# A fused sigmoid-attention and token-mixing kernel: eight load buffers instead of six, a re-planned instruction order, and the last output block in two PSUM banks

## The chip, the cores and the metric

The kernel runs on one core of a Trainium2 chip. The metric is device time in microseconds (us); lower is better. The core has five engines with queues of their own: PE (matrix multiplications; its weight loads are listed as PEld), DVE and ACT (element-wise work), POOL (element-wise work in SBUF) and SP (here it only issues DMAs). Work on one engine runs in program order; engines wait for one another through semaphores. PE writes PSUM, which has eight banks; DVE and ACT read PSUM and write SBUF.

## What is computed

```
scores = q @ k^T / sqrt(64) - log(448)      # 8 batches, 12 heads, 448 rows, 64 columns
attn   = sigmoid(scores)                    # no row sum: each element by itself
x      = attn @ v                           # -> 8 x 448 x 768, heads side by side
W      = (x @ w_q) @ (x @ w_k)^T / sqrt(64) # 448 x 448 for each batch
out    = relu(W @ x) @ w_out                # 8 x 448 x 768
```

The kernel computes W @ x as (x w_q) times ((x w_k)^T x), so that the 448 x 448 matrix is never formed. Inputs and output are float32 in HBM; the matrix work is done in bfloat16.

## The kernel before

**Tiling.** The 96 heads form 24 quads of four heads, three quads to a batch. A quad has q, k and v tiles of 128 x 896 float32 (448 KB each). Each is loaded by one SP DMA into a buffer of the pool `p_ld`, cast to bfloat16 (mostly on POOL, lines 178 and 188; a few on DVE), and q and k are brought into a transposed layout, by PE transposes with a copy out of PSUM (lines 202, 210, 272, 267) or by DVE transposes of SBUF tiles (lines 242, 249, 218).

**The stages, by the letter that stands for them.** `S` is one score step, 168 in all (seven for a quad): four PE matmuls into a pair of PSUM banks (line 284) and one ACT sigmoid over 128 x 896 elements (line 289). `P`/`p` is one step of attn @ v (line 302); after seven of them the sum leaves PSUM on DVE or, with the small letter, on ACT (line 311). `x`, `X`, `y` transpose the result (lines 325 and 342), `W`, `w`, `L`, `l` project it (six for a batch; `L` and `l` as four 64 x 64 matmuls whose halves are added afterwards, line 376; `W` and `w` as one 128 x 128 matmul, line 381), `N` and `U`/`T` form (x w_k)^T x, `M`/`m` multiplies by x w_q with the relu (line 438 on ACT, line 440 on DVE), and `O`, `o`, `I`, `i` are parts of the output product with w_out (lines 497, 534, 576), whose blocks are copied out of PSUM and stored to HBM. `F` is a filler matmul on zeros. Small letters mostly mean that the copy behind a step goes to ACT instead of DVE.

**Order.** All engines are ordered by hand: the string `PLAN` is read letter by letter, and each letter emits its instructions on all engines at once. No scheduler moves them afterwards. `PLAN` was made by a planner outside the kernel.

**Loads.** The string `ORDER` lists the loads. A load is issued as soon as the buffer that it reuses has been cast: `pump_loads` holds back load n until load n-6 has been cast, so six loads are under way or waiting at most. A dot ahead of a name gives its cast to DVE. Outputs are issued by SP too, in the same program order, so a load can stand behind an output that waits for its copy.

**PSUM.** Four pairs of banks are handed out from a free list. `bank1` gives one bank, `bank2` a pair. A block of `out_chunk` takes one bank: six matmuls of 128 x 384, then the copy. The last block of the kernel is copied by both engines: DVE takes 192 columns (line 597), ACT the other 192 (line 598), out of the same bank.

**Instruction streams.** PE's program is 7,464 weight loads and matmuls. DMA queue q8 brings it in pieces of 16 KB, 29 of them in this execution.

Of the kernel before, what the change touches and what calls it, by code (L numbers as in the profile page):

```python
# [17 lines left out]
def kernel(  # L18
# [12 lines left out]
    nc = tc.nc  # L31
# [6 lines left out]
    NU = B  # L38
    NJ = H // 4
    NC = D // P  # L40
    NB = D // 2
# [6 lines left out]
    def pool(name, bufs, **kw):  # L48
        return ctx.enter_context(tc.tile_pool(name=name, bufs=bufs, **kw))

    singles = pool("singles", 1)
    p_ld = pool("ld", 6)
    p_c16 = pool("c16", 2)
    p_v16 = pool("v16", 4)
    p_qk = pool("qk", 8)
# [16 lines left out]
    def bank2():  # L72
        n = free2.pop(0)
        return n, pairs[n], pairs16[n]

    def bank1():
        if halves:
            n, b = halves.pop(0)
        else:
            n, b = free2.pop(0), 0  # L80
            halves.append((n, 1))
        return (n, b), pairs[n][:, b], pairs16[n][:, b]

    def release(fb):
        if isinstance(fb, int):
            free2.append(fb)
        elif (fb[0], 1 - fb[1]) in halves:
            halves.remove((fb[0], 1 - fb[1]))
            free2.append(fb[0])
        else:  # L90
            halves.append(fb)
# [18 lines left out]
    def xt(u, j):  # L110
# [4 lines left out]


    PLAN = (
        "FFSSFKSSFqSFSkFSFFSFSPSappSPpSbSPPSSFqSSXSPSkSPppSprpSPPpSsP"
        "pPSXSPPSllSLzlLSPLpSpPSPPPSxSNSqkSUSpPSMpSppPSPSXSqkPSPppSWW"
        "SPPPSXSwMcSSwWWSppSPdxSpPPNSPSqkSMSSUpSpPSpMppSPSoSXSqkSOSMS"  # L120
        "ooMSSroopSsPPpSCPPPSooSzxOSOSLLcLSllLSpPpSpCpPdPSSOOSSoNxSOS"
        "xcSdUSPppSpPpSrPSoOSCPpSPsSPPpzSPOXoSMlLCSllLSLPpSpPPcpSPSdC"
        "OOSCSoXoSpMPScPppPSPSoOSxSdOXSppSppPpSPNooSMSUcdoSllxSLlLSLP"
        "pSPpPScPPodSoSMOSOSOrSOSMooPPsPSPxmpPPOSOSSOSzOOOSoNSOSUSPPx"
        "SpPMcpSppdllllScpPPpdLSlPOopSPooMeoSOSoSOOmoxSoNoSfTgPPSpppS"
        "POSPomOSOSooSoSOpSpPPSpocmepPoSooMlSLdLLSlLSOOSfgOSOSOoSxoSo"
        "PPxpSPpPSPoSoxSoSOSooSoNSOSTPpPSppSPPppMPppmpPylLlMLyllxiiiN"
        "iiUiimimImiiIoooOooOoOoooOooO"
    )
    PLAN = "".join(PLAN)  # L130
    KIND = ["a"] + [t for t in PLAN if t in "qacer"]
# [1 line left out]
    ld = {}  # L133
# [21 lines left out]
    def load1(n, nm, eng):  # L155
        u, j = quads[n]
        if KIND[n] in "cer" and nm != "v":
            t = p_ld.tile([P, 2 * NI * HD], F32, tag="ld", name=nm + "32")
            eng.dma_start(
                out=t, in_=SRC[nm][u, 4 * j : 4 * j + 4].rearrange("h (p r) d -> (h p) (r d)", r=2 * NI),  # L160
            )
            ld[nm, n] = t
            return
        t = p_ld.tile([P, 2, NI * HD], F32, tag="ld", name=nm + "32")
        eng.dma_start(
            out=t,
            in_=SRC[nm][u, 4 * j : 4 * j + 4].rearrange(
                "(g h) (p i) d -> (h p) g (i d)", g=2, i=NI
            ),
        )  # L170
        ld[nm, n] = t
# [304 lines left out]
    chunks = []  # L476
# [81 lines left out]
    def out_chunk(act, tail):  # L558

        if opened:  # L560
            w, m, nb, fb, ps = opened.pop()
            part = 1
        else:
            w, m, nb = chunks.pop(0)
            if nb < 0:
                nb = 0
                chunks.insert(0, (w, m, 1))
            fb, ps, _ = bank1()
            part = 0
        if nb == 0 and not part:  # L570
            ot[0] = p_o.tile([P, D], F32, tag="o", name="o")
        o = ot[0]

        def block(ps, w0, w1, c0, c1):
            for c in range(c0, c1):
                nc.tensor.matmul(  # L576
                    ps, mxs[w][:, 2 * S * c + m * P : 2 * S * c + (m + 1) * P],
                    wout16[:, c, w0:w1], start=(c == 0), stop=(c == NC - 1),
                )

        def store(cols):
            for y in range(2):
                b, i = divmod(2 * m + y, NI)
                eng = nc.scalar if tail and y else nc.sync
                eng.dma_start(
                    out=out[2 * w + b].rearrange("(p i) d -> p i d", i=NI)[:, i, cols],
                    in_=o[HALF[y], cols],
                )

        ps = ps[:, 0:NB] if not part else ps  # L590
        block(ps, nb * NB, (nb + 1) * NB, part * NC // 2, (part + 1) * NC // 2)
        if not part:
            opened.append((w, m, nb, fb, ps))
            return
        if w == NU // 2 - 1 and not chunks:
            h = NB // 2
            nc.vector.tensor_copy(out=o[:, NB : NB + h], in_=ps[:, 0:h])
            nc.scalar.copy(out=o[:, NB + h :], in_=ps[:, h:])
        else:
            COPY["s" if act else "v"](out=o[:, nb * NB : (nb + 1) * NB], in_=ps)  # L600
        release(fb)
        split = tail and w == NU // 2 - 1 and m == NI - 1
        if nb or split:
            store(slice(nb * NB, (nb + 1) * NB) if split else slice(0, D))
# [3 lines left out]
    def load_weights():  # L608
        w32["qk"] = p_ld.tile([P, 2 * NI * HD], F32, tag="ld", name="w32")[:, 0:D]
        for x, w in enumerate((moe_w_q, moe_w_k)):  # L610
            nc.sync.dma_start(
                out=w32["qk"].rearrange("p (c n) -> p c n", c=NC)[:, :, 64 * x : 64 * x + 64],
                in_=w.rearrange("(c p) n -> p c n", p=P)
            )

    def load_wout(c):
        w32[c] = p_ld.tile([P, 2 * NI * HD], F32, tag="ld", name="w32")[:, 0:D]
        nc.sync.dma_start(out=w32[c], in_=moe_w_out[c * P : (c + 1) * P, :])
# [9 lines left out]
    def cols(r):  # L628
        return slice(r.start * HD, r.stop * HD)
# [8 lines left out]
        out=ident, in_=ident, compare_op=ALU.not_equal, fill=1.0, base=0,  # L638
# [8 lines left out]
    for t in wqks:  # L647
# [1 line left out]


    ORDER = (
# [5 lines left out]
    )  # L657
    BY = {"s": [], "v": []}
    for x in ORDER.split():
# [9 lines left out]
    used, loaded, cast = set(), set(), set()  # L669

    ring = [("q", 0), ("k", 0)]

    def pump_loads():
        while len(loaded) < len(ORDER):
            nm, n = ORDER[len(loaded)]
            if len(ring) >= 6 and ring[-6] not in cast:
                break
            ring.append((nm, n))
            if nm == "w":
                load_wout(n - 1) if n else load_weights()  # L680
            else:
                load1(n, nm, nc.sync)
            loaded.add((nm, n))
            issued[nm, n] = done["S"]
# [55 lines left out]
    for t16, t32, r, e in ((q016, q0, IA, "v"), (q016, q0, IB, "s"), (k016, k0, KA, "g"), (k016, k0, KB, "g")):  # L740
        COPY[e](
            out=t16[:, r].rearrange("p i b d -> p b i d"),
            in_=t32[:, :, cols(r)].rearrange("p b (i d) -> p b i d", d=HD),
# [24 lines left out]
    for t in PLAN:  # L768
# [4 lines left out]
        c = done[kind]  # L773
# [29 lines left out]
        elif t == "K":  # L803
            tr_part("k", k016, KB, "v")
        elif kind == "x":
            tr_x(c, tail, t in "XY", "s" if t in "yY" else "v")
        elif kind == "W":
            mlp_wqk(*divmod(c, NC), tail, t in "wl", t in "Ll")
        elif kind == "C":
            for y in range(2):  # L810
                nc.sync.dma_start(out=wout16[HALF[y], NC + c, :], in_=wout16[HALF[1 - y], c, :])
        elif kind == "N":
            mlp_wkn(c)
        elif kind == "U":
            (mlp_tmp_tiled if t in "Tt" else mlp_tmp)(c, t in "ut")
        elif kind == "M":
            u, x = divmod(c, NC // 2)
            mlp_mix(u, x, t == "m", tail)
            if x == NC // 2 - 1:
                if u // 2 in TW:  # L820
                    chunks.extend((u // 2, ((u % 2, i), (u % 2, 6 - i))) for i in range(3))
                    if u % 2:
                        chunks.append((u // 2, ((0, 3), (1, 3))))
                else:
                    chunks.extend((u // 2, m, -1) for m in (range(3, NI) if u % 2 else range(3)))
        elif kind == "O":
            if (opened or chunks)[0][0] in TW:
                out_pair(t == "o")
            elif t in "Ii":
                out_halves(t == "i")  # L830
            else:
                out_chunk(t == "o", tail)
# [29 lines left out]
```

## Time and profile before

| what | value |
|---|---|
| median of 3 runs | 190.4 us (189.7 to 190.98) |
| profiled execution, its own time | 189.52 us |
| span of the profile in it | 187.7 us, so 1.82 us lie around it |
| PE busy | 175.9 us (94%) |
| ACT busy | 165.1 us (88%), of this 141.0 in 168 sigmoids |
| DVE / POOL busy | 137.8 us / 108.4 us |
| first sigmoid starts, last one ends | 6.62 us, 165.07 us |
| last matmul group (line 576) | 175.53 to 183.50 us |

Busy time says how long an engine had work under way; idle time is put down to what ended it (the releaser). "issue" as a releaser means that the engine waited for nothing that the profile shows. The chain of work that ended last is followed back from the end: at each step to what released it.

### The profile page before, as it was taken

What the parts mean: (1) busy time and instruction counts of PE and PEld (TensorE: products, weight loads), DVE (VectorE), ACT (ScalarE), POOL (GpSimd) and SP (SyncE); (2) the same over time, 40 slices, a digit from 0 to 9 for tenths busy, and PEclk for the clock granted to TensorE, in tenths of its full rate; (3) what the DMA queues carried; (4) which work ended last, traced back from release to release, by engine and by line L of the source; (5) the groups of instructions that cost most, each with busy time, mean ns of one, the idle gap of its engine ahead of it and who ended that gap; (6) DMA issues with size and microseconds to landing.
All of it is one profiled execution on the core that took longest, in us unless ns stands there. A gap on an engine that the chain in (4) does not pass through costs nothing.

```text
span 187.7 us, 8660 instructions
## 1 busy us (share of the span) xinstructions
PE 175.9 (94%) x3732; PEld 116.1 (62%) x3732; DVE 137.8 (73%) x208; ACT 165.1 (88%) x214; POOL 108.4 (58%) x145
## 2 busy tenths in 40 slices
PE   7999899899999999999999998998899999999990
PEld 7444556454554554555565785777787788886650
DVE  3254598589868998999889996897676966587700
ACT  4699999899999989999999999896899999995440
POOL 1526798995979389699999887846184310001000
PEclk9999999999999999999999999999999999999998
DMA  6999999969999698898999997599747936332485
GB/s 179 372 356 331 319 367 373 379 209 306 370 354 401 226 269 258 216 356 258 291 256 299 351 352 272 123 322 374 206 117 219 303 102 179 97 79 57 121 247 168
DMA packets 26390, 48.99 MB, mean 261 GB/s; under 512 B 4080, under 2 KB 20208, under 8 KB 26352
## 3 DMA queue, kind: packets, MB, share of 16 engines
q1 hardware_dynamic: 25952, 47.65, 78.0%
q10 hardware_dynamic: 400, 0.79, 1.3%
q8 instruction: 29, 0.48, 1.0%
q14 instruction: 9, 0.07, 0.2%
HBM read 35.78 MB, written 11.01 MB: 249 GB/s over the span
## 4 chain that ended last, share of the span: by engine, by line
PE 74%; DVE 10%; ACT 9%; issue 4%; DVEq 0%; ACTq 0%
PE banks L497 15%; PE banks L284 15%; PE banks L302 13%; PE banks L576 10%; ACT at L289 9%; PE banks L368 4%; PE banks L534 3%; DVE xt L311 3%; PE banks L412 2%; PE banks L342 2%; DVE qk L218 2%; PE banks L644 2%; DVE qk L272 2%; PE banks L452 1%; PE banks L202 1%
## 5 line engine op out<-in xcount | busy, mean ns | idle before, releaser
L289 ACT ACTIVATE at<-banks 128x896 bf16<-128x896 f32 x168 | 141.0, 939 | 7.0 <-PE banks L284 6.2
L284 PE MATMUL banks<-qk 64*64 64x448 bf16 x672 | 65.0, 358 | 2.0 <-ACT at L289 0.9
L302 PE MATMUL banks<-at,v 64*64 64x448 bf16 x672 | 48.0, 351 | 1.2 <-issue 0.7
L284 PEld LDWEIGHTS <-qk 64*64 64x64 bf16 x672 | 27.4, 105 | 21.8 <-issue 11.6
L497 PE MATMUL banks<-wout,mx 64*64 64x384 bf16 x672 | 36.9, 323 | 2.0 <-issue 2.0
L302 PEld LDWEIGHTS <-v 64*64 64x64 bf16 x672 | 22.7, 107 | 9.8 <-issue 3.5
L497 PEld LDWEIGHTS <-mx 64*64 64x64 bf16 x672 | 24.1, 107 | 6.4 <-issue 2.2
L188 POOL CAST v<-v 128x896 bf16<-128x896 f32 x23 | 21.8, 951 | 8.1 <-DMA v<-in_v_dram 7.6
L311 DVE CAST xt<-banks 128x896 bf16<-128x896 f32 x21 | 22.6, 1078 | 5.1 <-PE banks L302 4.3
L576 PE MATMUL banks<-wout,mx 128*128 128x384 bf16 x132 | 25.0, 327 | 0.1
L178 POOL CAST qk<-k 128x896 bf16<-128x896 f32 x14 | 16.7, 1193 | 13.7 <-DVE mv L253 4.6
L440 DVE TENSOR_SCALAR mx<-banks 128x1024 bf16<-128x1024 f32 (+2 forms) x20 | 19.9, 1001 | 3.7 <-PE banks L464 2.1
L576 PEld LDWEIGHTS <-mx 128*128 128x128 bf16 x132 | 11.5, 97 | 10.9 <-issue 4.9
L377 POOL COPY wq<-wqk 64x448 bf16<-64x448 bf16 x7 | 3.9, 555 | 20.1 <-DVE wqk L376 19.8
L178 POOL CAST qk<-q 128x896 bf16<-128x896 f32 x11 | 13.6, 1238 | 3.0 <-DMA q<-in_q_dram 1.4
L249 DVE STREAM_TRANSPOSE qk<-qk 128x448 f32<-128x448 f32 x24 | 14.6, 626 | 0.0
L355 DVE COPY xn<-banks 128x1024 bf16<-128x1024 bf16 (+1 forms) x16 | 10.2, 637 | 4.2 <-PE banks L342 4.1
L153 POOL COPY qk<-swap 32x448 uint32<-32x448 uint32 x20 | 12.1, 605 | 1.2
L506 DVE COPY o<-banks 128x768 f32<-128x768 f32 x9 | 8.6, 958 | 5.2 <-PE banks L497 3.5
L147 POOL COPY swap<-qk 32x448 uint32<-32x448 uint32 x20 | 11.1, 554 | 1.8 <-DVE qk L178 0.7
L368 PE MATMUL banks<-xt,wqk 64*64 64x448 bf16 x168 | 11.9, 351 | 0.2
L150 POOL COPY qk<-qk 32x448 uint32<-32x448 uint32 x20 | 11.1, 554 | 1.2
(88 smaller groups left out, 224.7 us busy)
## 6 DMA issues: line engine op xcount, KB each, us to landing
q<-in_q_dram SPq DMA_DIRECT2D x24, 448.0 KB, 5.9
v<-in_v_dram SPq DMA_DIRECT2D x24, 448.0 KB, 6.1
k<-in_k_dram SPq DMA_DIRECT2D x23, 448.0 KB, 6.0
out_dram<-o SPq DMA_DIRECT2D x51, 192.0 KB, 3.8
w<-in_moe_w_out_dram SPq DMA_DIRECT2D x6, 384.0 KB, 5.7
wout<-wout SPq DMA_DIRECT2D x12, 96.0 KB, 4.8
out_dram<-o ACTq DMA_DIRECT2D x3, 192.0 KB, 3.5
qk<-mv SPq DMA_DIRECT2D x8, 56.0 KB, 2.6
```

The source lines that it names most:

```text
L153: eng.tensor_copy(out=w[lo, 1], in_=z[lo])
L178: COPY[e](out=f[:, :, "qk".index(nm)].rearrange("p e i d y -> p e y i d"), in_=ld.pop((nm, n)).rearrange("p (y i e d) -> p e y i d", y=2, ...
L188: COPY[e](out=t16.rearrange("p i b d -> p b i d"), in_=ld.pop((nm, n)).rearrange("p b (i d) -> p b i d", i=NI),)
L249: nc.vector.transpose(out=qk[n][:, t].rearrange("p t i n -> p (t i n)").bitcast(F32), in_=w)
L284: nc.tensor.matmul(sc[HALF[h], g, 0:S], qk[n][HALF[g], h, 1, i, :], qk[n][HALF[g], h, 0].rearrange("p i n -> p (i n)"), start=True, stop=True,
L289: nc.scalar.activation(at, sc[:, :, 0:S], ACTF.Sigmoid, bias=attn_bias, scale=attn_scale)
L302: nc.tensor.matmul(ps[HALF[g], h, 0:S], ld["v16", n][HALF[h], i, g, :], ats[n, i][HALF[h], g, :], start=(i == 0), stop=(i == NI - 1),)
L311: COPY[eng](out=xt(u, j)[:, :, 0:S], in_=ps[:, :, 0:S])
L368: nc.tensor.matmul(ps[HALF[x], y, 0:S], wqk16[HALF[y], c, 64 * x : 64 * x + 64], xt(u, c // 2)[HALF[y], c % 2, 0:S], start=(c == 0), stop= ...
L440: nc.vector.tensor_scalar(dst, ps, moe_scale, 0.0, ALU.mult, ALU.max)
L497: nc.tensor.matmul(ps[HALF[x], y, 0:NB], mx[HALF[y], u, b, 64 * (i - 3 * y) : 64 * (i - 3 * y) + 64], wout16[HALF[y], slot(y, b), x * NB : ...
L576: nc.tensor.matmul(ps, mxs[w][:, 2 * S * c + m * P : 2 * S * c + (m + 1) * P], wout16[:, c, w0:w1], start=(c == 0), stop=(c == NC - 1),)
```

## The change

- `p_ld` has eight buffers, and `pump_loads` holds back load n until load n-8 has been cast.
- `PLAN` and `ORDER` are new strings. The same stages with the same counts are ordered anew (168 S, 168 P, 112 output parts, 48 projection parts and so on). 30 projection parts are tiled instead of 42, so 18 are whole instead of 6; 10 transposes of x are whole instead of 8. v0 is loaded ahead of q2. PE has 156 instructions fewer.
- The title of the change says that the new plan was made "with instruction fetches that wait longer behind queued loads". No line of the diff sets this; it is read here as a figure that the planner reckoned with.
- The last output block takes a pair of banks. Each of its six steps becomes two matmuls of 128 x 192, one into each bank. DVE then copies one bank, ACT the other.

```
-    p_ld = pool("ld", 6)
+    p_ld = pool("ld", 8)
...
-        "FFSSFKSSFqSFSkFSFFSFSPSappSPpSbSPPSSFqSSXSPSkSPppSprpSPPpSsP"
...
-        "PPxpSPpPSPoSoxSoSOSooSoNSOSTPpPSppSPPppMPppmpPylLlMLyllxiiiN"
-        "iiUiimimImiiIoooOooOoOoooOooO"
+        "FFSSFKSSFSqFSSkFFFSSSSSFpPpqPSkPSPPPSPSPSabSSPPxSPPrPSppSSXp"
...
+        "SOppSPPPSPSPoOSONSOoSOSxOSOStpPPSpppPpPmlpmPpPpLMLlyxLLIiIxN"
+        "iiUiIMiMImiiiOoOOOoOoOOooOooOo"
...
-            fb, ps, _ = bank1()
+            fb, ps, _ = bank2() if w == NU // 2 - 1 and not chunks else bank1()
             part = 0
+        last = isinstance(fb, int)
...
-        ps = ps[:, 0:NB] if not part else ps
-        block(ps, nb * NB, (nb + 1) * NB, part * NC // 2, (part + 1) * NC // 2)
+        ps = ps if last or part else ps[:, 0:NB]
+        if last:
+            for c in range(part * NC // 2, (part + 1) * NC // 2):
+                for x in range(2):
+                    block(ps[:, x, 0 : NB // 2], NB + x * NB // 2, NB + (x + 1) * NB // 2, c, c + 1)
+        else:
+            block(ps, nb * NB, (nb + 1) * NB, part * NC // 2, (part + 1) * NC // 2)
...
-            nc.vector.tensor_copy(out=o[:, NB : NB + h], in_=ps[:, 0:h])
-            nc.scalar.copy(out=o[:, NB + h :], in_=ps[:, h:])
+            nc.vector.tensor_copy(out=o[:, NB : NB + h], in_=ps[:, 0, 0:h])
+            nc.scalar.copy(out=o[:, NB + h :], in_=ps[:, 1, 0:h])
...
-        "q1 k1 .q2 v0 .k2 q3 v1 q4 k3 k4 v2 w0 v3 k5 v4 q5 "
...
+        "q1 k1 .v0 q2 .k2 v1 q3 k3 q4 v2 k4 w0 v3 .q7 k5 q5 "
...
-            if len(ring) >= 6 and ring[-6] not in cast:
+            if len(ring) >= 8 and ring[-8] not in cast:
```

More of the change, by code (lines that the diff above doesn't have):

```diff
@@ L117 @@
     PLAN = (
-        "FFSSFKSSFqSFSkFSFFSFSPSappSPpSbSPPSSFqSSXSPSkSPppSprpSPPpSsP"
[L119 to L126, printed above, removed]
-        "PPxpSPpPSPoSoxSoSOSooSoNSOSTPpPSppSPPppMPppmpPylLlMLyllxiiiN"
-        "iiUiimimImiiIoooOooOoOoooOooO"
+        "FFSSFKSSFSqFSSkFFFSSSSSFpPpqPSkPSPPPSPSPSabSSPPxSPPrPSppSSXp"
+        "PSpPSSsFzSSWXwWWWWpSppPSpNpSPSqSkSUSSPXPSPpPSqkSpPSMSSPpPpSS"
+        "ppPSWXWSSqkwSXSMWSwWSppMSpSpppcNSPSdUSxSSPppMSppPPSSqkSXSoSS"
+        "OOroSMsSOoPSpMpSppppSozwOWSSSwOOwWWSppcpSpxpSCPdPSoSNOSxSUSp"
+        "PpScpSdpPPSrOOSSsOOzSpPPSpPpSSPOXoSMLlSlLClSLPpPSPpcpCSPSOod"
+        "OSxSXoSMpPCCpScpPpSCPSdoOSppPSpSoXSPpSPooNSMcSUoxSldlLSllLSp"
+        "pppSPcpPSOSdoMSOOSOSOSPOrSsOPmPpzpmppxOoSONSOSoocSxSOOSSUPSP"
+        "cPPMSPSPPSllLSldPLpSpLppmpXpoMSoSdoOScOSONSOOSOSodxSoSoPSpPe"
+        "PTpPOSPOmoMSoofOSPPePSogSoPPpfPSoogSOoMSLLLLSLLSoOSOOSoSOxSo"
+        "SOppSPPPSPSPOoSONSOoSOSxOSOStpPPSpppPpPmlpmPpPpLMLlyxLLIiIxN"
+        "iiUiIMiMImiiiOoOOOoOoOOooOoOo"
     )
@@ L594, in out_chunk @@
             return
-        if w == NU // 2 - 1 and not chunks:
+        if last:
             h = NB // 2
-            nc.vector.tensor_copy(out=o[:, NB : NB + h], in_=ps[:, 0:h])
-            nc.scalar.copy(out=o[:, NB + h :], in_=ps[:, h:])
+            nc.vector.tensor_copy(out=o[:, NB : NB + h], in_=ps[:, 0, 0:h])
+            nc.scalar.copy(out=o[:, NB + h :], in_=ps[:, 1, 0:h])
         else:
```

8 rows, old and new, of the table ORDER are left out of this document.

## The prediction

> **What bounds the kernel now.** The page first: busy shares, the 40 slices, and the chain that ended last.
>
> ```profile
> PE 175.9 (94%) x3732; PEld 116.1 (62%) x3732; DVE 137.8 (73%) x208; ACT 165.1 (88%) x214; POOL 108.4 (58%) x145
> ...
> PEclk9999999999999999999999999999999999999998
> DMA  6999999969999698898999997599747936332485
> ...
> PE 74%; DVE 10%; ACT 9%; issue 4%; DVEq 0%; ACTq 0%
> ```
>
> The clock is full throughout, so no term comes from it. PE and ACT are both nearly full, POOL has no part in the chain, and 4% of the chain (7.5 us) is "issue", PE waiting for nothing that the profile shows. The table of stretches tells which engine is full where (stretch, its length, then busy PE, PEld, DVE, ACT, POOL, clock, DMA share, GB/s):
>
> ```profile
> 20.00:30.00 10.00, 9.39 (x192) 5.89 (x191) 8.63 (x13) 9.94 (x13) 8.28 (x11) 1.00 1.03 350
> 50.00:60.00 10.00, 9.52 (x172) 5.09 (x175) 7.51 (x9) 10.00 (x14) 8.33 (x10) 1.00 1.00 366
> 120.00:130.00 10.00, 9.31 (x227) 7.01 (x227) 8.28 (x12) 8.19 (x11) 5.73 (x9) 1.00 1.00 320
> 170.00:180.00 10.00, 10.00 (x150) 6.38 (x141) 6.29 (x13) 4.57 (x10) 0.00 (x0) 1.00 0.50 124
> ```
>
> To about 100 us ACT is the bound; from 105 us the chain is nearly all PE, with ACT close behind; from 165 us, when the last sigmoid ends, PE works off the outputs alone. So the time is 6.62 us to the first sigmoid, 158.45 us of sigmoids, and 22.6 us from the last sigmoid to the end.
>
> Then PE's own timeline, for waits of over half a microsecond with "issue" as their end (start, duration, what, idle before):
>
> ```profile
> 36.87 0.57 PE L302 MATMUL banks<-at,v 64*64 64x448 bf16 x7 [0.75 <-issue]
> 115.94 0.64 PE L497 MATMUL banks<-wout,mx 64*64 64x384 bf16 x9 [0.74 <-issue]
> 127.44 0.32 PE L497 MATMUL banks<-wout,mx 64*64 64x384 bf16 x1 [0.69 <-issue]
> ```
>
> A fourth, 0.58 us, ends at 133.37. I counted PE's weight loads and matmuls in the trace: all four gaps stand 192 instructions behind a multiple of 256. Queue q8 brings PE's program in 29 pieces of 16 KB (256 instructions of 64 bytes), and in its packet records the piece due at each of these points had landed only 0.3 to 0.5 us before PE stopped there. So these are late instruction fetches. If a fetch is triggered some 200 instructions after the last boundary (the earliest place at which any of the 29 begins), those four waited 3.1 to 3.7 us before their packet began, while the ones from 134 to 170 us, where DMA is half idle, waited about 1 us. ACT paid behind each:
>
> ```profile
> 37.73 2.54 ACT L289 ACTIVATE at<-banks 128x896 bf16<-128x896 f32 x3 [0.76 <-PE banks L284]
> 128.24 0.92 ACT L289 ACTIVATE at<-banks 128x896 bf16<-128x896 f32 x1 [1.39 <-PE banks L284]
> ```
>
> With 0.73 at 118.53 and 0.68 at 134.49 that is 3.6 us of ACT's 5.9 us idle between the first and last sigmoid.
>
> **The change, part by part.** The base is the profiled execution: 189.52 us, span 187.7.
>
> *Buffers.* What they can save is waiting for loads: POOL idles 7.6 us for v, 3.8 for q at line 188, 1.4 and 1.8 at line 178. None of it is on the chain, and no ACT idle names POOL or DMA after the first sigmoid. I price it at 0: POOL's slack (58% busy) hides it today as well. At the start SP issues six loads in a row behind the first quad's three pieces instead of four, 0.5 us each; they stand behind the pieces on the same queue: 0. They do change when DMA is full, which is the next but one item.
>
> *The order.* Same stages, so what counts is what stands in front of the last sigmoid on ACT and behind it on PE.
> - ACT, in front of it, besides 168 sigmoids. Before: 7 copies of 384 columns at 0.486, 5 of 768 at 0.798, 4 relus at 1.040, one xt copy at 0.900, one wpart at 0.586: 13.04 us. After: 7, 4, 4, three xt copies and one upart (no such row on ACT; 0.48 by the 128x384 copy at line 539): 13.93 us. That is +0.9, nearly all of it within the first 98 score steps, where ACT is the bound. I take +0.9; the low end is 0, if it falls into ACT's idle time behind PE at 66.67, 85.03 and 100.01 (0.57, 0.34 and 0.31).
> - PE, behind it: 11 attn @ v letters instead of 9, the rest equal in count (6 projections, 12 `I`, 16 `O`). Sixteen matmuls of line 302 take 0.76 in the chain, so two letters are 0.38 us more. They are missing in front of the last sigmoid, where PE is also full: +0.38 if ACT sets the last sigmoid's time, 0 if PE does. I take 0, as PE sets it from 105 us on in the chain.
> - I priced every letter by its chain row (`S`, `P` and projections 0.19, output parts 0.49, `U` 0.75) and summed for stretches of quads, PE against ACT. Quads 15 to 17: before 18.7 and 19.1, after 18.2 and 19.1. Quads 18 to 20: 24.7 and 23.0, after 21.7 and 22.5. Quads 21 to 24: 27.3 and 27.2, after 29.4 and 27.7. The larger of each adds up to 71.1 before and 71.0 after: 0.
> - Whole instead of tiled projections: six letters of line 368 take 1.14 in the chain (0.57 for three) and three of line 381 take 0.67, so 12 more whole ones cost PE between 0 and +0.4; two units fewer with an addition save DVE 1.3 us (0.617 + 0.625 against 0.586 each), off the chain. Within the bounds: 0.
>
> *Fetches.* PE has 156 instructions fewer, so 28 or 29 pieces as now. What matters is which of them are triggered while loads queue and have less PE work than they need: 3.1 to 3.7 of wait, 0.9 to 1.1 of transfer, and 1.4 from landing to PE's restart make 5.5 to 6. I counted the new plan's instructions to the same points (192 behind each multiple of 256). Pieces 4, 6, 16 and 19 have windows of six or fewer score steps or much output work (some 5 us) just behind bursts of casts, which let loads out; 4, 16, 18 and 19 had that before. Same number, so 0. Bounds: all four gone, -2.8 of PE's idle time; four more of 0.7 each, +2.8.
>
> Does a deeper ring lengthen a wait? Against it: at 9.8, 18.0 and 24.6 us, with three to four loads out by issues against bytes moved, the fetch waited 2.3 to 2.9; at 110.6 and 127.7, with about two out, 3.1 and 3.6. The wait does not grow with the depth beyond that. The Trainium skill, page "DMA: Bandwidth & Descriptors", section "Queues, rings and completion order", says that each DMA engine takes turns between the queues that have work and switches after a packet of descriptors. By that rule a fetch would never stand behind the whole ring, and two more buffers would add 0. It agrees with the flat waits, not with 3.7 us against 1, so the trace bears it out in part only. Its page "Runtime: NRT & Kernel Launch", section "Instruction fetch mechanics", has PE refilled in blocks of 256 instructions, which the 256-step agrees with, and calls the crossing mostly hidden; here 4 of 29 were not.
>
> *Last block.* Today DVE's half starts at 183.59, then ACT's, which waits for it:
>
> ```profile
> 183.59 0.36 DVE L597 COPY o<-banks 128x192 f32<-128x192 f32 x1 [5.35 <-PE banks L576]
> 183.99 0.32 ACT L598 COPY o<-banks 128x192 f32<-128x192 f32 x1 [0.80 <-DVE o L597]
> 184.33 0.50 ACTq L585 DMA_DIRECT2D out_dram<-o  x1
> ```
>
> With a bank each they start together: -0.40. On PE twelve matmuls of 192 columns replace six of 384. 48 of the latter take 7.97, 0.166 each; half the columns at half the price is 0. The other end is the weight load, 0.097 on line 576: 12 x 0.097 is 1.16 against 1.00, +0.17. Seven loads and transposes of 128 columns on line 210 take 0.55 to 0.56, 0.08 a pair, so I take +0.05. A pair of banks is free by then, as nothing but output blocks holds PSUM. Sum: -0.35.
>
> **Sum.** +0.9 - 0.35 = +0.55: span 188.25, 190.07 us against the base's own 189.52. The base is 0.9 below the median of the runs. Since that is within their scatter, I put the forecast between 190.07 and 190.4 + 0.55 = 190.95: **190.5 us**, no change.
>
> **Rivals.**
> 1. *Slower: loads are under way at more boundaries.* Eight buffers let bursts run longer, so more of the fetches between 40 and 140 us start behind loads. Place: pieces 5, 6, 13 to 19. Price: the measured gap, 0.7 on PE and up to 1.4 on ACT. It decides once a fetch waits over about 2.5 us where PE needs 5 us for its 246 instructions. With four more such gaps 190.5 + 2.8 = 193.3; if waits also grew by 8/6, 1.2 us each on some five, up to 196. For it: four gaps already, all where DMA is full; against: flat waits. Chance 0.28.
> 2. *Faster: the new plan lays its boundaries where PE has slack.* No gap of over half a microsecond: -2.8, and the ACT time +0.9 vanishes in idle: 190.5 - 2.8 - 0.5 = 187.2; half of it gives 188.8. For it: the sums show room, since quads 18 to 20 carry 3 us less PE work; against: quads 21 to 24 take it back, and the dense output parts use 24 instructions in 0.49 us. Chance 0.24.
> 3. *The buffers do nothing:* casts wait for their bfloat16 buffers, not for loads, and only the order and the last block act. 190.1 to 190.5, inside the forecast.
>
> **Numbers.** Forecast 0.48, slower 0.28, faster 0.24. The range holds half of each rival: 187.8 to 193.6. A measurement of this kernel can hardly tell less than 1%, 1.9 us, from no change. Faster by over 1% 0.24, within 0.48, slower 0.28.
>
> **What would show it.** In the new profile: waits for DMA on POOL shorter by several us with the span unmoved; the line of ACT's last copy without a wait for DVE, 0.3 to 0.4 us between the last matmul and the last store; three to five "issue" gaps on PE of over half a microsecond, all 192 behind a multiple of 256; ACT busy about 0.3 us more in all, its last sigmoid ending near 166. More gaps, or longer ones, is rival 1; none is rival 2. The forecast falls too if DVE, with two casts more, comes late with a quad's transposes and ACT idles behind it.

## The result, and the profile after

The changed kernel takes 190.06 us (median of 22 runs, 189.02 to 192.19), the kernel before 189.72 us in the same sessions (22 runs, 188.50 to 190.98). The ratio is **1.0063, 95% interval 1.0038 to 1.0087**: about 0.6% slower, inside the 1% either way that the prediction calls no change. The profiled execution took 189.71 us with a span of 187.9 (before: 189.52 and 187.7).

The page of the changed kernel, the lines that answer to those shown of before:

```profile
PE 174.7 (93%) x3652; PEld 115.3 (61%) x3654; DVE 138.5 (74%) x208; ACT 165.6 (88%) x214; POOL 106.2 (57%) x143
...
PEclk9999999999999999999999999999999999999999
DMA  5999999998999969899979945997498547332585
...
PE 68%; ACT 14%; DVE 6%; issue 5%; DMA 3%; ACTq 1%; SPq 0%; POOL 0%; DVEq 0%
```

The clock is full as before, and the same two engines are full. The table of stretches (stretch, length, then busy PE, PEld, DVE, ACT, POOL, clock, DMA share, GB/s):

```profile
20.00:30.00 10.00, 9.02 (x156) 4.84 (x158) 8.33 (x12) 9.70 (x12) 7.71 (x11) 1.00 1.06 371
50.00:60.00 10.00, 9.59 (x214) 5.22 (x207) 7.73 (x12) 9.99 (x14) 9.71 (x13) 1.00 0.97 352
100.00:110.00 10.00, 8.80 (x203) 5.84 (x203) 8.26 (x12) 8.10 (x11) 8.57 (x11) 1.00 0.93 316
120.00:130.00 10.00, 9.60 (x199) 6.85 (x192) 8.49 (x11) 9.94 (x13) 5.77 (x9) 1.00 1.01 349
170.00:180.00 10.00, 10.00 (x151) 6.38 (x143) 5.92 (x12) 5.19 (x12) 0.00 (x0) 1.00 0.51 129
```

From 120 to 130 us ACT is full now, where it had 8.19 us of work before. The place where both engines lose time has moved to 100 to 110 us, where the kernel before lost nothing:

```profile
100.00:110.00 10.00, 10.00 (x237) 7.00 (x231) 9.45 (x14) 9.99 (x13) 8.41 (x12) 1.00 0.96 329
```

PE's timeline of the changed kernel (start, duration, what, idle before and what ended it) has only one wait of over half a microsecond with "issue" as its end, and two short ones for DVE behind it:

```profile
108.64 0.81 PE L497 MATMUL banks<-wout,mx 64*64 64x384 bf16 x13 [1.20 <-issue]
...
117.22 1.17 PE L497 MATMUL banks<-wout,mx 64*64 64x384 bf16 x24 [0.19 <-DVE wkn L403]
...
123.99 0.38 PE L284 MATMUL banks<-qk 64*64 64x448 bf16 x4 [0.34 <-DVE mx L440]
```

The gap of 1.20 us stands 192 instructions behind a multiple of 256, as all four did before (the trace counts 190 and lacks two of PE's 7,308 records), and costs ACT 1.75 us on its own timeline:

```profile
109.73 0.92 ACT L289 ACTIVATE at<-banks 128x896 bf16<-128x896 f32 x1 [1.75 <-PE banks L284]
```

The end of the kernel, on DVE's and ACT's timelines:

```profile
183.59 0.36 DVE L603 COPY o<-banks 128x192 f32<-128x192 f32 x1 [2.35 <-PE banks L577]
183.83 0.32 ACT L604 COPY o<-banks 128x192 f32<-128x192 f32 x1 [0.57 <-PE banks L577]
184.18 0.50 ACTq L586 DMA_DIRECT2D out_dram<-o  x1
```

ACT's copy waits for PE instead of DVE, and starts at 183.83 instead of 183.99.

Cutting each span at three points shows where the time lies. "Gaps" is the sum of PE's waits over 0.3 us that end in "issue"; they lie in the second column. The last column leaves out the start: it runs from the 15th sigmoid, the first of the third quad, to the last one's end. The other rows are the experiments below.

| kernel | first sigmoid starts | to last sigmoid's end | to last matmul's end | to the end | gaps | from the 15th sigmoid to the last one's end |
|---|---|---|---|---|---|---|
| before | 6.62 | 158.45 | 18.44 | 4.23 | 2.76 (4) | 147.28 |
| changed | 6.33 | 158.20 | 19.05 | 4.35 | 1.20 (1) | 146.39 |
| before, eight buffers | 6.9 | 159.80 | 18.44 | 4.16 | 3.29 (4) | 148.62 |
| before, ten buffers | 6.5 | 160.01 | 18.55 | 4.16 | 3.52 (4) | 148.83 |
| before, two banks at the end | 8.2 | 157.75 | 18.67 | 4.34 | 1.85 (3) | 146.31 |
| before, half the load bytes | 6.5 | 155.67 | 18.44 | 4.17 | none | 143.88 |
| before, 16 warm-up matmuls fewer | 7.2 | 157.59 | 18.44 | 4.43 | 1.97 (3) | 146.42 |
| changed, six buffers | 7.2 | 164.22 | 19.04 | 4.38 | 0.94 (1) | 152.72 |
| changed, half the load bytes | 6.5 | 156.10 | 19.05 | 4.34 | none | 144.70 |
| changed, 16 warm-up matmuls fewer | 7.2 | 158.07 | 19.05 | 4.36 | 0.73 (1) | 146.43 |
| changed, one bank at the end | 6.6 | 158.58 | 19.03 | 4.20 | 1.17 (2) | 145.94 |
| changed, k20 cast on POOL | 6.8 | 157.69 | 19.05 | 4.32 | 1.75 (2) | 146.29 |
| the same, one bank at the end | 6.5 | 158.58 | 19.03 | 4.17 | 2.21 (2) | 146.64 |
| the same, two banks, half the load bytes | 6.5 | 155.48 | 19.04 | 4.38 | none | 143.91 |

The first column varies by up to 1.9 us from one execution to another. That is more than most of the effects looked for, so single spans are not compared below: the columns are, and the ratios of timed runs. The second column has a part of this chance in it still: in five of the fourteen executions PE waits 0.75 to 1.82 us for POOL's cast of the first k right behind the first sigmoid.

The last column is steadier, and quad by quad (from a quad's first sigmoid on ACT to the next quad's; quads are counted from 1 here) two executions of one order agree to 0.1 us in most quads. From the third quad on, the kernel before with full loads and with half the load bytes differs by more in five quads only: with full loads it loses 0.93, 1.05, 0.95 and 0.78 us in quads 6, 18, 19 and 20, each of which holds one of the four gaps, and regains 0.34 in quad 22. So effects of some tenths of a microsecond can be read quad by quad, though whole runs scatter by 3 us.

### The profile page after: what moved, and what is told of

Same layout as the page of the kernel before. It is cut to its first block, busy times and chain, and to the rows that moved or that the text cites. A ratio compares the mean times of both kernels' runs of the same rounds, so it can differ in the third digit from the quotient of the medians.

```text
span 187.9 us, 8501 instructions
## 1 busy us (share of the span) xinstructions
PE 174.7 (93%) x3652; PEld 115.3 (61%) x3654; DVE 138.5 (74%) x208; ACT 165.6 (88%) x214; POOL 106.2 (57%) x143
## 4 chain that ended last, share of the span: by engine, by line
PE 68%; ACT 14%; DVE 6%; issue 5%; DMA 3%; ACTq 1%; SPq 0%; POOL 0%; DVEq 0%
PE banks L497 14%; ACT at L289 14%; PE banks L284 14%; PE banks L302 12%; PE banks L577 11%; PE banks L534 3%; PE banks L368 3%; DMA k<-in_k_dram 3%; PE banks L342 2%; DVE mx L440 2%; DVE qk L218 2%; PE banks L325 2%; PE banks L412 2%; PE banks L452 1%; DVE xt L311 1%
## 5 line engine op out<-in xcount | busy, mean ns | idle before, releaser
L284 PE MATMUL banks<-qk 64*64 64x448 bf16 x672 | 62.8, 358 | 3.2 <-ACT at L289 0.9
L284 PEld LDWEIGHTS <-qk 64*64 64x64 bf16 x672 | 25.9, 105 | 22.6 <-issue 14.1
L577 PE MATMUL banks<-wout,mx 128*128 128x384 bf16 (+1 forms) x138 | 24.7, 320 | 0.2 <-DVE mx L440 0.2
L188 POOL CAST v<-v 128x896 bf16<-128x896 f32 x22 | 20.4, 932 | 4.5 <-DMA v<-in_v_dram 3.4
L311 DVE CAST xt<-banks 128x896 bf16<-128x896 f32 x19 | 20.6, 1083 | 3.0 <-PE banks L302 2.4
L178 POOL CAST qk<-q 128x896 bf16<-128x896 f32 x13 | 15.8, 1216 | 5.8 <-DMA q<-in_q_dram 3.4
L377 POOL COPY wq<-wqk 64x448 bf16<-64x448 bf16 x5 | 2.8, 554 | 26.1 <-DVE wqk L376 26.0
L178 POOL CAST qk<-k 128x896 bf16<-128x896 f32 x11 | 13.6, 1246 | 4.4 <-DVE qk L249 2.9
L272 DVE COPY qk<-banks 128x1792 bf16<-128x1792 bf16 x6 | 6.5, 1088 | 7.3 <-ACT at L289 3.7
L355 DVE COPY xn<-banks 128x1024 bf16<-128x1024 bf16 (+1 forms) x14 | 8.7, 629 | 2.9 <-PE banks L342 2.7
```

The source lines that it names most:

```text
L178: COPY[e](out=f[:, :, "qk".index(nm)].rearrange("p e i d y -> p e y i d"), in_=ld.pop((nm, n)).rearrange("p (y i e d) -> p e y i d", y=2, ...
L188: COPY[e](out=t16.rearrange("p i b d -> p b i d"), in_=ld.pop((nm, n)).rearrange("p b (i d) -> p b i d", i=NI),)
L284: nc.tensor.matmul(sc[HALF[h], g, 0:S], qk[n][HALF[g], h, 1, i, :], qk[n][HALF[g], h, 0].rearrange("p i n -> p (i n)"), start=True, stop=True,
L311: COPY[eng](out=xt(u, j)[:, :, 0:S], in_=ps[:, :, 0:S])
L577: nc.tensor.matmul(ps, mxs[w][:, 2 * S * c + m * P : 2 * S * c + (m + 1) * P], wout16[:, c, w0:w1], start=(c == 0), stop=(c == NC - 1),)
```

## The experiments

Each ratio is to the kernel before on the same chip, with its 95% interval.

### Eight buffers alone, and ten

The kernel before with nothing but the buffers changed (ten likewise):

```
-    p_ld = pool("ld", 6)
+    p_ld = pool("ld", 8)
...
-            if len(ring) >= 6 and ring[-6] not in cast:
+            if len(ring) >= 8 and ring[-8] not in cast:
```

> The kernel before with eight load buffers alone: the same instructions in the same order, only loads are let out two earlier. Theory A (the prediction's: a fetch's wait does not grow with the loads that are out beyond three): the gaps of PE stay about 0.6 to 0.75 us, ratio to before 0.997 to 1.003. Theory B (the wait grows with the loads that are queued, as the changed kernel's first three pieces suggest, 3.6 to 4.0 us with five to six loads out against 2.3 to 2.9 with three to four): the first fetches wait 3.5 to 4 us, one to four gaps get longer by 0.3 to 1 us, ratio 1.002 to 1.010.

> The kernel before with ten load buffers alone. Theory A: as with eight, ratio 0.997 to 1.003, waits not over 4 us. Theory B: the first fetches wait 4.5 to 5.5 us, gaps at the start of the kernel too, ratio 1.005 to 1.020 and above that of eight buffers.

Eight: **1.0136** [1.0093, 1.0178]. Ten: 1.0112 [1.0057, 1.0167]. Buffers alone make the old order slower, eight by more than either theory had it, and ten are not worse than eight, though theory B had them so. PE's timeline with eight:

```profile
116.40 0.65 PE L497 MATMUL banks<-wout,mx 64*64 64x384 bf16 x9 [0.62 <-issue]
...
128.47 0.32 PE L497 MATMUL banks<-wout,mx 64*64 64x384 bf16 x1 [1.26 <-issue]
...
142.02 0.38 PE L284 MATMUL banks<-qk 64*64 64x448 bf16 x4 [0.39 <-DVE xt L311]
```

The gap at 127.44 grew from 0.69 to 1.26, and the four together from 2.76 to 3.29. The wait at 142.02 is new, and has another cause: the place at which DVE's casts stand in its program depends on when their loads are let out, so eight buffers put v22's cast ahead of a copy that PE needs. So this is not quite the old order. Quad by quad, ACT loses 0.56 us more than before in quad 19, where the gap grew, 0.57 in quad 21, where the cast is in the way, and 0.27 in quad 7, which I did not trace; together they make up the +1.35 in the second column.

How long do fetches wait? By the packet records of q8, with what SP had issued and not yet moved when they were triggered, in loads of 448 KB:

| | three earliest fetches, us of wait | loads out at them | longest wait |
|---|---|---|---|
| six buffers, old order | 2.85, 2.31, 2.43 | 4.2 to 4.7 | 3.7 |
| eight, old order | 3.10, 2.81, 3.71 | 5.0 to 6.3 | 4.24 |
| ten, old order | 3.11, 3.53, 3.32 | 5.2 to 7.5 | 3.78 |
| changed kernel | 3.63, 4.00, 3.60 | 5.8 to 6.3 | 4.74 |
| changed kernel with six buffers | 1.99, 3.69, 3.71 | 3.8 to 5.0 | 4.38 |

These waits count from an assumed trigger, 200 instructions behind the last boundary. In the old order they grow by 0.3 to 1.3 us from six to eight buffers, and show no clear growth from eight to ten. But its fourth fetch waits 3.68, 3.72 and 3.49 us with six, eight and ten, and the new order reaches 3.7 us with six as well. So depth does not act in proportion, and which loads are out at a fetch seems to matter as much; this was not tested by itself.

### The changed kernel with six buffers

```
-    p_ld = pool("ld", 8)
+    p_ld = pool("ld", 6)
...
-            if len(ring) >= 8 and ring[-8] not in cast:
+            if len(ring) >= 6 and ring[-6] not in cast:
```

> The changed kernel with six load buffers again: its order and its last block, without the longer ring. If the longer ring is what costs (theory B), the gap of 1.20 us on PE at 108.6 us shrinks below 0.8 us and the ratio to before falls to 0.997 to 1.003. If the order costs by itself (0.9 us more of ACT work ahead of the last sigmoid, as the prediction had it), the ratio stays at 1.004 to 1.008. If the new order needs its eight buffers, POOL waits for loads and the ratio rises above 1.008.

**1.0322** [1.0263, 1.0381]: the slowest of all. Its chain, and the wait that stands in it, on POOL's and ACT's timelines:

```profile
PE 50%; ACT 14%; DMA 13%; DVE 12%; issue 4%; POOL 3%; SPq 1%; ACTq 1%; POOLq 0%; DVEq 0%
```

```profile
121.67 0.93 POOL L188 CAST v<-v 128x896 bf16<-128x896 f32 x1 [6.12 <-DMA v<-in_v_dram]
...
129.37 0.92 ACT L289 ACTIVATE at<-banks 128x896 bf16<-128x896 f32 x1 [3.39 <-PE banks L284]
```

DMA takes 13% of the chain, and POOL waits 10.9 us for v (3.4 with eight buffers). The third of the three outcomes named beforehand came about: with six buffers v comes too late for this order, and the two extra buffers cure that. In the old order POOL's waits (7.6 us for v) are not on the chain; here the same kind of wait is.

### Half the bytes of every load

q, k and v loads bring half of their bytes and each cast reads that half twice. This leaves out half of q, k and v; instructions and element counts stay.

```
-                out=t, in_=SRC[nm][u, 4 * j : 4 * j + 4].rearrange("h (p r) d -> (h p) (r d)", r=2 * NI),
+                out=t[:, 0 : NI * HD],
+                in_=SRC[nm][u, 4 * j : 4 * j + 4].rearrange("h (p r) d -> (h p) (r d)", r=2 * NI)[:, 0 : NI * HD],
...
-            in_=ld.pop((nm, n)).rearrange("p b (i d) -> p b i d", i=NI),
+            in_=ld.pop((nm, n))[:, 0:1].to_broadcast([P, 2, NI * HD]).rearrange("p b (i d) -> p b i d", i=NI),
```

> The kernel before with the q, k and v loads cut to half their bytes (each tile's second half is not loaded; the casts read the first half twice), so half of the inputs is left out; instructions and their order are the same. If loads queued ahead of a fetch make PE's gaps (192 instructions behind a multiple of 256), these gaps vanish or stay under 0.2 us, fetches wait about 1 to 1.5 us, ACT's idle time falls by some 3 us and the time by 1.5 to 3 us: ratio 0.984 to 0.992. If the gaps have another cause, they stay and the ratio is 0.997 to 1.001.

> The changed kernel with the q, k and v loads cut to half their bytes in the same way. With fetches no longer late, what is left between it and the kernel before with half loads is the order's own worth: by the prediction's sum (+0.9 us of ACT work, -0.35 us at the end) it is 0.3% slower than that; if the longer ring's fetches are what cost, it is equal or up to 0.5% faster. Ratio to the kernel before 0.982 to 0.994; its gap of 1.20 us at 108.6 us is gone.

The kernel before so altered: **0.9846** [0.9795, 0.9896]. The changed kernel: **0.9949** [0.9913, 0.9986]. Neither has an "issue" gap over 0.3 us left, and their fetches mostly wait about 1 us. Two readings follow.

First, the loads' price. In the old order the second column falls by 2.78 us (158.45 to 155.67), and the gaps were 2.76. That the two agree so closely is partly luck, as PE waited 1.24 us for the first k in the execution with half the bytes. Without the start (last column) the old order pays 3.40 us. All but 0.1 of what it loses lies in the four quads that hold a gap, so a gap of 0.6 to 0.75 us on PE costs ACT 0.8 to 1.05. Two other executions of the old order with six buffers fit: 2.43 us lost with 1.85 of gaps, and 2.54 with 1.97. So with six buffers the old order pays for its loads almost wholly through late instruction fetches. The new order pays 1.69 (146.39 to 144.70), half as much, partly because k20's cast (below) costs it less with full loads.

Second, the order's own price, with loads out of the way. It is 1.0% by the two ratios, more than the 0.3% expected, and 1.5 us by the medians (187.84 and 186.34, taken together). The profiles give +0.82 from the 15th sigmoid to the last, +0.61 behind it and +0.17 at the end. Of the +0.82, 0.49 lie between the 15th sigmoid and quad 17, whose first sigmoid starts at 104.11 instead of 104.02: 86.24 us instead of 85.75. With full loads and no late fetch in that stretch it is 85.8 in the old order (two executions) and 86.1 to 86.4 in the new one (four). The rest comes behind. From 104 to 120 us, the kernel before and the changed one, both with half the bytes:

```profile
104.00:120.00 16.00, 16.00 (x420) 12.33 (x412) 15.16 (x20) 15.64 (x20) 13.14 (x17) 1.00 0.67 187
```

```profile
104.00:120.00 16.00, 15.34 (x401) 11.87 (x396) 14.64 (x21) 14.85 (x19) 14.43 (x21) 1.00 0.62 178
```

PE is full in the first and idles 0.66 us in the second, where ACT loses 0.79. PE's timeline of the second names the cause, DVE's shows what stood in the way (line numbers are three higher in these kernels):

```profile
115.68 1.17 PE L500 MATMUL banks<-wout,mx 64*64 64x384 bf16 x24 [0.59 <-DVE wkn L406]
...
122.45 0.38 PE L287 MATMUL banks<-qk 64*64 64x448 bf16 x4 [0.34 <-DVE mx L443]
```

```profile
114.00 1.45 DVE L179 CAST qk<-k 128x896 bf16<-128x896 f32 x1
115.35 0.27 DVE L406 COPY wkn<-banks 128x256 bf16<-128x256 bf16 x1
```

PE's output matmuls do not read `wkn`. In the program this copy empties a PSUM bank and then gives it free, so what they wait for must be the bank. The copy could not start until DVE had finished casting k20. In the old order DVE casts k20 in front of the same copy:

```profile
116.81 1.32 DVE L179 CAST qk<-k 128x896 bf16<-128x896 f32 x1
118.03 0.27 DVE L406 COPY wkn<-banks 128x256 bf16<-128x256 bf16 x1
```

But there PE is full throughout, so the same cast costs nothing.

### k20's cast on POOL

In the function that emits one cast:

```
-    cast_now(nm, n, e)
+    cast_now(nm, n, "g" if (nm, n) == ("k", 20) else e)
```

> The changed kernel with half loads and with the cast of k20 moved from DVE to POOL, at the same place of the program. Between the two kernels with half loads, where no fetch is late, PE of the new order waits 0.59 us at 115.7 us for DVE's copy of wkn, which stands behind that cast (1.45 us), and 0.34 us at 122.5 us for DVE's relu. If this DVE cast is what the new order loses by, the wait of 0.59 us falls below 0.2 us and the ratio to before falls from 0.9949 by 0.2 to 0.4%, to 0.991 to 0.993. If the loss is spread over the order (ACT's 0.9 us more, two letters more behind the last sigmoid), the wait may go but the ratio stays at 0.994 to 0.996.

> The changed kernel with full loads and the cast of k20 moved from DVE to POOL. With full loads PE's wait for wkn is 0.19 us in the profile, as the late fetch at 108.6 us holds PE back ahead of it. So the gain is 0 to 0.5 us: ratio to before 1.003 to 1.007, against 1.0063 of the changed kernel. Slower than that would say that the cast is late on POOL.

With half loads 0.9900 [0.9867, 0.9933] against 0.9949 [0.9913, 0.9986] without the edit, a little more than expected. The wait of 0.59 is gone, and of PE's waits over 0.3 us between 112 and 126 us one is left:

```profile
121.82 0.38 PE L287 MATMUL banks<-qk 64*64 64x448 bf16 x4 [0.34 <-DVE mx L443]
```

Quad 19's first sigmoid starts 0.63 us sooner (118.95 instead of 119.58). Quad by quad, the two executions agree to 0.02 us from the third quad on, except for one: quad 18, which holds the wait, is 0.79 us shorter. That is the price of this cast with half loads, 0.4%.

With full loads the ratio is **0.9999** [0.9960, 1.0039] against the changed kernel's 1.0063 [1.0038, 1.0087], a larger gain than the 0 to 0.5 us expected. The intervals just touch. The profiled span shows nothing of it, 187.9 both, because that execution had more late fetches:

```profile
108.57 0.81 PE L497 MATMUL banks<-wout,mx 64*64 64x384 bf16 x13 [1.24 <-issue]
...
145.61 1.00 PE L497 MATMUL banks<-wout,mx 64*64 64x384 bf16 x19 [0.51 <-issue]
```

Here too quad 18 tells the cast's price. Against the execution with half loads and k20 on POOL it is 0.42 us longer in the changed kernel, 0.42 in the same with one bank, and 0.80 in the changed kernel with 16 warm-up matmuls fewer (below); with k20 on POOL it is not longer in either execution with full loads. How long the cast takes goes with it: 1.05 us in the first two, where PE waits 0.19 for `wkn`, and 1.47 in the third, where it waits 0.50:

```profile
117.44 1.17 PE L497 MATMUL banks<-wout,mx 64*64 64x384 bf16 x24 [0.50 <-DVE wkn L403]
```

(With six buffers the cast takes 0.68 us, PE does not wait for `wkn`, and quad 18 is 0.05 us longer.) So in the changed order with eight buffers the cast costs 0.4 to 0.8 us, 0.2 to 0.4%. The ratios, 0.5% and 0.6%, are higher but no sharper than about 0.5% either way. So this cast is a third to two thirds of the measured loss of 1.2 us. What is left of the order's own price, 0.9900 against 0.9846, lies behind the last sigmoid (+0.60 and, at the end, +0.21), not between the 15th sigmoid and the last (+0.03): the 0.49 us lost up to quad 17 are won back behind it.

### The fetch boundaries moved

16 of the 32 warm-up matmuls at the start of PE's program are left out, in the changed kernel and in the one before, so that every boundary falls on other work.

```
-    for _ in range(32):
+    for _ in range(16):
```

> The changed kernel with 16 of the 32 warm-up matmuls at the start left out, 32 instructions, so that every boundary between instruction pieces falls 32 instructions later in the plan. If the gap at 108.6 us is a late fetch, it moves 32 instructions later in the plan, and as its trigger then comes some 0.8 us later behind loads issued up to 100.7 us, it gets 0.5 to 0.8 us shorter; ratio to before 0.999 to 1.006. If gaps belong to the plan's own places, they stay where they are. The first sigmoid should start at the same time, since PE waits for q there.

> The kernel before with 16 of its 32 warm-up matmuls left out, so that all 29 boundaries of PE's program fall 32 instructions later in the plan. By the theory of late fetches, a trigger that comes 0.7 to 0.8 us later finds 0.7 us less of the same loads ahead of it at pieces 4, 16, 18 and 19, whose loads were issued before the trigger: each of the four gaps gets shorter by about that, from 2.8 us in all to under 1.2 us, and the ratio is 0.990 to 0.997. If other loads come in between, some gaps stay and new ones appear, 0.997 to 1.004. If gaps have to do with places of the plan and not with fetches, nothing changes.

Changed: 1.0088 [1.0048, 1.0127]. Before: 1.0014 [0.9965, 1.0063]. Both make no clear difference, though the gaps moved; the first is above the range expected, the second in the one for new gaps in the place of old ones. The changed kernel's timeline, then that of before:

```profile
38.99 0.23 PE L202 MATMUL banks<-ident,q 64*64 64x64 bf16 x5 [0.73 <-issue]
...
109.39 0.68 PE L497 MATMUL banks<-wout,mx 64*64 64x384 bf16 x12
```

```profile
111.31 0.32 PE L497 MATMUL banks<-wout,mx 64*64 64x384 bf16 x1 [0.41 <-issue]
116.68 1.62 PE L497 MATMUL banks<-wout,mx 64*64 64x384 bf16 x33 [0.60 <-issue]
133.34 0.39 PE L342 MATMUL banks<-ident,xt 64*64 64x64 bf16 x25 [0.96 <-issue]
```

In the first, the gap of 1.20 near 109 us is gone and one of 0.73 stands at 38.99. In the second, the gaps at 36.87 and 127.44 are gone, a new one stands at 111.31, and the one at 133 is longer. Each boundary stays 192 behind a multiple of 256. The gaps follow the instruction count, not the work, and moving them exchanges one for another. Which ones come late also varies where the order in front of them is the same: the changed kernel has one gap of 1.20 us near 109 us, and with one bank at its end 0.49 there and 0.68 at 146.32.

### The last block

The two-bank block alone, in the kernel before (the hunks of `out_chunk` in the diff), and the changed kernel with these hunks undone:

```
-            fb, ps, _ = bank1()
+            fb, ps, _ = bank2() if w == NU // 2 - 1 and not chunks else bank1()
```

> The kernel before with its last output block in two banks alone. The prediction's term: ACT's half starts 0.40 us earlier, at DVE's start, and PE's last block is 0.05 us longer, -0.35 us. By the changed kernel's profile: ACT's half starts 0.24 us behind DVE's, as its bank is finished by the last matmul of all, so -0.15 us. Both lie within the scatter of the ratio, 0.997 to 1.002; the profile tells them apart by the start of ACT's copy against DVE's.

> The changed kernel with its last output block in one bank again: order and ring of the change alone. If the two banks are worth 0.15 us, the ratio is 1.005 to 1.010, not to be told from the changed kernel's 1.0063; if they cost (twelve shorter matmuls, two more waits), 1.002 to 1.006. In the profile ACT's half starts 0.40 us behind DVE's.

Alone: 0.9981 [0.9947, 1.0015]. Undone: 1.0027 [0.9983, 1.0071] against 1.0063 [1.0038, 1.0087] with it. Neither tells a gain or a loss. The profile says why there is none. The end of the first kernel:

```profile
184.61 0.36 DVE L603 COPY o<-banks 128x192 f32<-128x192 f32 x1 [5.28 <-PE banks L577]
184.85 0.32 ACT L604 COPY o<-banks 128x192 f32<-128x192 f32 x1 [0.57 <-PE banks L577]
```

| us behind the last matmul | one bank | two banks |
|---|---|---|
| DVE's copy starts | 0.09 | 0.01 |
| ACT's copy starts | 0.48 | 0.25 |
| last store issued | 0.83 | 0.59 |
| last packet of SP's store ends | 2.6 to 2.7 | 2.82 to 2.87 |
| program ends | 4.16 to 4.23 | 4.32 to 4.38 |

(One execution of a one-bank kernel is outside: 2.97 and 4.43, the shifted kernel of before.) The last store goes out 0.24 us sooner, and the program ends 0.1 to 0.2 us later. ACT does not start with DVE even so: its bank is the one that the last matmul closes.

### Both edits of the changed kernel together

k20's cast on POOL and one bank at the end, both as above.

> The changed kernel with the cast of k20 on POOL and with its last block in one bank again: the two findings together, as a candidate to beat both kernels. Six profiles put the end of the program 4.2 us behind the last matmul with one bank and 4.35 with two, so one bank should gain 0.1 us: ratio to before 0.997 to 1.001, below the changed kernel's 1.0063 and not to be told from the one with k20 alone (0.9999). If two banks do gain, it is above 1.001.

**0.9965** [0.9925, 1.0005], with 2.21 us of gaps in the profiled execution. The best version found. Its median is 0.7 us below that of the changed kernel (taken in other sessions; the intervals of the ratios, 0.9925 to 1.0005 and 1.0038 to 1.0087, do not meet), and it can't be told from the one before.

## Why the prediction was right, and where its steps were not

The forecast was 190.5 us and no change; it came out at 190.06 and +0.6%. The sum of +0.55 us stands against +0.2 in the profiled executions and +1.2 by the ratio (0.0063 x 189.7). The total was right because errors of both signs cancelled, and which fetches come late is partly chance. In the two profiled executions the +0.2 is made up of +0.36 up to the 15th sigmoid (the start, which varies by more than that in either order), -1.3 from late fetches, +0.42 from k20's cast, nothing from the rest of the order up to the last sigmoid, +0.61 behind it and +0.12 at the end. Of the prediction's steps only some held.

- **Buffers, 0: wrong as a term by itself.** They cost the old order 1.4%, and the new order without them is 3.2% slower than the kernel before. POOL's waits for v fell from 7.6 to 3.4 us with the span unmoved, as said (those for q at line 178 rose from 1.4 to 3.4). But "POOL's slack hides it" holds for the old order only: the new one had been laid on eight buffers. The two parts can't be priced one at a time.
- **ACT +0.9, low end 0: between the two.** ACT's busy time rose by 0.5. From the 15th sigmoid to quad 17, where ACT is the bound, the new order takes 0.2 to 0.7 us more in every execution without a late fetch there. That the extra copies are the cause fits, but was not tested.
- **The sums by quads, 0, and the DVE term that was missing.** PE and ACT were summed letter by letter, DVE was not. "The forecast falls too if DVE, with two casts more, comes late" was named as a risk without a price; it is the step that failed. DVE's cast of k20, 1.05 to 1.47 us in front of a copy of 0.27, costs 0.4 to 0.8 us, and with it on POOL the changed kernel comes to 0.9999. What waits is PE for a PSUM bank, and ACT behind it, not a quad's transposes as the risk had it. A sum over a stretch can't see this, since DVE is only 74% busy; it takes the order of instructions on that one engine.
- **Two letters behind the last sigmoid, 0.** The third column is some 0.6 longer in all versions of the new order, more than the 0.38 of two letters. The last sigmoid came at 164.5, not near 166. With late fetches and k20's cast out of the way the stretch from quad 17 to the last sigmoid is 0.46 shorter (57.67 instead of 58.13). So most of it was paid back in front of the last sigmoid, as the 0 had it, where it made up for ACT's loss; which letters make up the rest I did not test.
- **Fetches, same number, 0: wrong in count.** One gap instead of four, 1.20 us instead of 2.76. That is 1.56 of rival 2's 2.8, and it paid for k20's cast and the longer tail. (Rival 2 takes 0.5 off for ACT where its words say 0.9; with 0.9 its sum is 186.8, not 187.2.) "The wait does not grow with the depth beyond that" fell in part: the early fetches wait 3.6 to 4.0 us instead of 2.3 to 2.9, but ten buffers are no worse than eight, and the new order has waits of 3.7 with six. Rival 1's proportional growth fell too. The rule of alternating queues (the Trainium skill, "DMA: Bandwidth & Descriptors", section "Queues, rings and completion order"), by which two more buffers would add 0, agrees with eight against ten, and with the three earliest fetches not with six against eight. That a crossing is mostly hidden (the Trainium skill, "Runtime: NRT & Kernel Launch", section "Instruction fetch mechanics") agrees with the half-byte kernels, where none shows.
- **Last block, -0.35: wrong.** The start of ACT's copy gained 0.16 to 0.24 instead of 0.40, because its bank is closed by the last matmul of all; the last store is issued 0.59 us behind that matmul, not 0.3 to 0.4, and nothing of the gain reached the end.

## What to carry to other kernels

When both main engines are full, a new order by hand must be walked through on the third engine as well: one cast of 1.05 to 1.47 us, in front of a small copy that gives PE its bank, cost 0.4 to 0.8 us and so up to two thirds of what this change lost. A deeper load ring and the order made for it are one edit: each alone lost more (1.4% and 3.2%) than the two together. And before a change is credited with tenths of a per cent, look at where the instruction fetches fell: this kernel, which queues loads most of the time, has gaps that an edit of PE's program moves about. Compare two traces of one order stage by stage: here they agree to hundredths of a microsecond in most quads, so what differs stands out.

## What was not expected of the hardware

- Late instruction fetches were nearly the whole price of the loads in the old order: 3.40 us from the 15th sigmoid to the last, all but 0.1 of the losses in quads with one of the four gaps, and 1.5% of the run. Every gap looked at stood 192 instructions behind a multiple of 256. The fetches in front of a gap had waited 2.8 to 5.2 us, by the assumed trigger; some others waited over 3 us without one. With half the load bytes most waited about 1 us or less. In the changed kernel the piece that waited 4.74 had landed 1.4 us before PE went on.
- Loads, and with them probably the late fetches, also make the scatter: eleven of twelve runs of the changed kernel with half the bytes lie between 187.73 and 188.66 us, while with full loads its 22 runs spread over 3.2 us.
- Stores issued 0.24 us sooner did not land sooner. With two banks the last packets of both engines' stores end about 2.85 us behind the last matmul, and with one bank SP's end at 2.6 to 2.7. Why is open.
